# Making one shifted copy of every eighth batch with an adding DMA instead of VectorE

## The chip, the cores and the metric

The kernel runs on one core of a Trainium2 chip. Five engines matter: TensorE (PE in the profile, with its weight loads as PEld), ScalarE (ACT), VectorE (DVE), GpSimd (POOL) and SyncE (SP), which issues most of the DMAs. Each engine works through its own queue in the order in which the program wrote it; an engine whose next instruction waits for a semaphore does nothing else meanwhile. The metric is the device time of one execution in microseconds.

## The reference

Two attention branches read the same input and are mixed by a gate. Only branch A matters for the change: plain softmax attention over 2048 tokens with 32 heads of 16 dimensions.

```python
def _A_ref(x, wqkv, wo):
    B, S, D = x.shape          # 1, 2048, 512
    H = 32; Dh = D // H        # 16
    qkv = (x @ wqkv) ...       # q, k, v: (B, H, S, Dh)
    scores = jnp.einsum("bhqd,bhkd->bhqk", q, k) * (Dh ** -0.5)
    p = _softmax(scores, axis=-1)
    o = jnp.einsum("bhqk,bhkd->bhqd", p, v)
    return o_as_tokens @ wo

g = _sigmoid((x * gate_w).sum(-1, keepdims=True))
a = _A_ref(x, A_wqkv, A_wo)
b = _B_ref(x, B_wqkv, B_w_phi, B_wo)   # linear attention with softmax features
return g * a + (1 - g) * b
```

The work is dominated by the exponentials of branch A: 32 heads x 2048 x 2048 scores.

## The kernel before

**Units, packs and groups.** Branch A is cut into 2048 units: one unit is the score tile of one head for 128 keys and 512 queries (128 x 512 values, one PSUM bank). Four units with the same keys make a pack (four heads on the four strips of the array), 16 packs (2048 keys) make a group, and there are 32 groups of 64 units. For each unit PE makes the scores (`_scores`, L1040), some engine turns them into exponentials, and PE multiplies these with the values and adds the result into the group's accumulator bank (`_values`, L1147). At the end of a group the accumulator is transposed on DVE (L1168) and normalised, and sixteen small DMAs with a transpose behind them (L1191, L1195) put it into `onTA` for the output projection.

**Two ways to an exponential.** Most units (1544 of 2048) go through ACT: scores of two units at a time lie in two of the four ring banks 0 to 3, one ACTIVATE (L1088) makes both exponentials into the ring `ET`, which has `NSLOT` slots of one unit each, and a values matmul (`_pv`) of a whole pack frees its slots. An exponential waits for the values matmul of the unit `NSLOT` places before it.

The other 504 units go through DVE, spread over the groups by the list `NUMS` (6 in the first group, up to 21 in a late one). They are taken in batches of four (`PACK`), 126 in all, by `_vector_batch`. A batch goes like this:

1. Four score matmuls (named `vqk`), each into a free bank of 4 to 7, and per unit one DVE instruction (L946, named `v_bits`) that multiplies by a scale, adds an origin and writes 16-bit integers: read as bf16 these are a first power of two with a straight line between powers. They fill `va[:, 0]`, a tile of 128 x 4 x 512.
2. One DVE instruction (L971 with k = 1, named `v_step`) writes `va[:, 1] = va[:, 0] + 31`, a copy shifted by 31 in the integers, form 128x2048.
3. One DVE instruction (L971 with k = 2) writes `vs[:, :] = va[:, :] + 64`, both halves at once, form 128x4096.
4. Four values groups on PE (named `pvx`), one for each of the four shifted tiles, the first two with `V` and the last two with `V2`, a copy of the values scaled by 0.703125. The sum of the four is the exponential to the precision wanted.

There are two `va` tiles (`NA` = 2, batch number modulo 2) and two `vs` tiles. A batch may write its `va` tile only when the batch two before has been read from it: by its own values groups and by its k = 2 step. A batch is meant to begin seven packs (`LEAD`) before its first unit's turn.

Between these lie the projections of both branches and all of branch B, on PE, DVE, ACT and POOL.

**What sets the order.** A planner (`Plan.order`) simulates the five queues with a cost for each operation (`cost`), a latency until its result is seen elsewhere (`lat`), priorities (`prio`) and times before which it may not run (`rel`). At each step it takes the operation that can start first, and among those about as early the one with the lowest rank. Score matmuls of ACT's units come first on PE. A `pvx` or `pv` becomes urgent some packs after its unit's turn (`URGENT` = 4). PE's gaps are filled with matmuls of a zero tile (L1154). The planner knows that POOL's instructions and certain DVE instructions (`PORT`, among them `v_step`) exclude each other (`o.port`). In `shift`, each operation's priority gets a small random-looking offset that depends on its name, on its running number among operations of that name, and on a list of 34 seeds. The resulting order of every queue is then written out with semaphore waits (`emit`).

All DMAs before the change are issued from SP, except for five from ACT at the start and the end. A large load has a planned cost of 0.5 us on its queue and a latency of its own: 8.0 for `WB`, 4.5 for `WoB`, 4.0 for `WoA`. The sixteen small DMAs of L1191 are one planned operation of 11.0 us on SP.

Of the kernel before, what the change touches and what calls it, by code (L numbers as in the profile page):

```python
# [7 lines left out]
ALU = mybir.AluOpType  # L8
AX = mybir.AxisListType

P = 128
# [4 lines left out]
QCH = 512  # L16
SCALE = float(DH) ** -0.5
F32, BF16 = dt.float32, dt.bfloat16
U16, FP16 = dt.uint16, dt.float16
LOG2E = 1.4426950408889634  # L20
STEPS, RATIO, ORIGIN = (31, 64), 0.703125, 127 * 128 - 279
# [18 lines left out]
class Op:  # L40
    def __init__(self, eng, fn, cost, name, prio, rel, kind, lat):
        self.eng, self.fn, self.cost, self.name = eng, fn, cost, name
        self.prio, self.rel, self.kind, self.lat = prio, rel, kind, lat
        self.deps = []
        self.users = []
        self.left = 0
        self.need = False
        self.acquire = None
        self.release = None
        self.also = None  # L50
        self.twin = None
        self.sem = None
        self.start = self.end = None
        self.on_commit = None
        self.array = 0.0
        self.filler = 0
        self.pad = False
        self.filled = 0
        self.strips = None
        self.urgent = 1 << 30  # L60
        self.held = self.port = False
        self.alone = -99
        self.group = None


class Plan:
# [43 lines left out]
    def op(self, eng, fn, cost, reads=(), writes=(), deps=(), name="", prio=0.0, rel=-99, kind="full",  # L110
           acquire=None, release=None, lat=None, array=None, strips=None, also=None):
        o = Op(eng, fn, cost, name, prio, rel, kind, self.LAT[eng] if lat is None else lat)
        found = {}
        for b in reads:
            for w in b.writers:
                found[id(w)] = w
        for b in writes:
            for w in b.readers or b.writers:
                found[id(w)] = w
            if b.readers:  # L120
                for w in b.writers:
                    found[id(w)] = w
        for d in deps:
            if d is not None:
                found[id(d)] = d
        found.pop(id(o), None)
        o.deps = list(found.values())
        for b in reads:
            b.readers.append(o)
        for b in writes:  # L130
            b.writers, b.readers = [o], []
        o.acquire, o.release, o.also = acquire, release, also
        o.strips = strips
        o.port = eng == "POOL" or eng == "DVE" and name in self.PORT
        o.held = eng == "PE" and acquire is None and name in self.HOLDING
        o.array = cost if array is None else array
        self.ops.append(o)
        return o
# [187 lines left out]
    def emit(self, nc, ctx):  # L326
        sems = {e: ctx.enter_context(nc.semaphore(f"done_{e}")) for e in self.ENGS if e != "SP"}
        for q in self.queues.values():
            for o in q:
                for d in o.deps:  # L330
                    if not (d.eng == o.eng == "PE"):
                        d.need = True
        count = dict.fromkeys(self.ENGS, 0)
        for e, q in self.queues.items():
            for o in q:
                if o.name.startswith("dma"):
                    o.sem = (ctx.enter_context(nc.semaphore(o.name)), 16 * len(o.fn) if isinstance(o.fn, list) else 16)
                elif o.need:
                    count[e] += 1
                    o.sem = (sems[e], count[e])  # L340
# [67 lines left out]
class _Kernel:  # L408
    NRING = 4
    GROUPS = (2, 2)  # L410
    NSLOT = 22
    PACK, PAIRS, PAIR0 = 4, 0, 0
    VCP = 8 * 17
    NQS = 4
# [21 lines left out]
    PADK = 2  # L436
    LAST, FIRST_OUT, NEXT_OUT, DEP_OUT = 0, 3, 0, 2
    ALONE, EARLY = 12, 10
    PVP = 10

    def __init__(self, nc, A_x, A_wqkv, A_wo, B_wqkv, B_w_phi, B_wo, gate_w, out):
# [33 lines left out]
    def _memory(self, ctx):  # L475
        nc, S, NT, NQC = self.nc, self.S, self.NT, self.NQC
# [65 lines left out]
        self.outt = self.WB[:, 0:2, 2 * D:3 * D]  # L542
        tiles = [sb(f"vs{k}", [P, 2, self.PACK, QCH], U16) for k in range(self.NST + self.NA)]
        self.vs, self.va = tiles[:self.NST], tiles[self.NST:]
        self.sbuf_used = at[0]


# [58 lines left out]
    def _consts(self):  # L606
        op = self.plan.op
        B = Buf
        self.b_iden, self.b_mask = B(), B()
        self.b_V = [[B() for _ in range(self.NT // 2)] for _ in range(4)]  # L610
        self.b_V2 = [[B() for _ in range(self.NT // 2)] for _ in range(4)]
        self.early = {}
        self.b_VB = [B() for _ in range(4)]
        op("POOL", lambda e: e.memset(self.iden[:], 0.0), 0.25, writes=[self.b_iden], prio=-90)
        op("POOL", lambda e: e.affine_select(
# [9 lines left out]
        n = 4 * self.NT * self.VCP  # L625
# [294 lines left out]
    def _vector_batch(self, number, units, due):  # L920
# [45 lines left out]
        vs, b_vs, b_vb = self.vs[slot], self.b_vs[slot], self.b_vb[number % self.NA]  # L966
        for k in range(4):
            tile, buf = (vs if k > 1 else va)[:, k % 2], b_vs if k > 1 else b_vb if k else b_va
            if k in (1, 2):
                src, dst = (va[:, 0, 0:n], va[:, 1, 0:n]) if k == 1 else (va[:, :, 0:n], vs[:, :, 0:n])  # L970
                o = op("DVE", lambda e, k=k, src=src, dst=dst: e.tensor_scalar(dst, src, float(STEPS[k - 1]), None,  # L971
                                                                               op0=ALU.add),
                       0.16 + k * n * QCH * 0.00026, reads=[b_va] + [b_vb] * (k - 1), writes=[buf], name="v_step",
                       prio=units[0] / 4 - 4)
                o.urgent = units[0] // 4 - self.AHEAD + 2
            v, bufs = (self.V, self.b_V) if k < 2 else (self.V2, self.b_V2)
            for g in sorted({u // (4 * NT) for u in units}):
# [11 lines left out]
                self.late.setdefault(g, []).append(x)  # L989
                if g in self.opened:  # L990
                    x.deps.append(self.opened[g])

    def _attention(self):
        plan, NT, NQC = self.plan, self.NT, self.NQC
# [704 lines left out]
```

## Time and profile before

| | |
|---|---|
| times of the runs | 757.13 and 758.5 us, median 757.82 |
| span of the profiled execution | 755.8 us, about 2 us less than the median of the runs, since a run's time also has what lies around the span |
| ACT busy | 741.1 us (98%) |
| PE busy | 744.3 us (98%) |
| DVE busy | 719.9 us (95%) |
| POOL busy | 228.6 us (30%) |
| granted clock of TensorE | 1.00 throughout |
| chain that ended last | ACT 69%, PE 18%, DVE 11%, DMA 1% |

A line of the profile names the line of the kernel (L971), the engine, the operation, the tiles written and read (`vs<-vs`; the tiles `va` go by the name `vs` there, since they are allocated from one list), the form (partitions x elements) and a count. Idle time of an engine that isn't the bottleneck costs nothing. Since matmuls overlap, a busy PE is not a PE at its limit. Neighbouring instructions of ACT and DVE overlap a little, so the distance between two starts tells more than a duration.

### The profile page before, as it was taken

Reading aid. Unit: us, or ns where it says so; the run is one execution under the profiler, and the core shown is the slowest. Engines: PE = TensorE matmul, PEld = TensorE weight load, DVE = VectorE, ACT = ScalarE, POOL = GpSimd, SP = SyncE. Lnnn points to the kernel's source line nnn. Section 1 sums busy time; section 2 is a strip of 40 time slices with the busy share of each in tenths; the row PEclk is TensorE's granted clock in tenths of the full one; section 3 lists DMA queues with packets and bytes.
Section 4 is the critical chain, followed back from the end, with each engine's and each line's share of the span. In section 5 each row is a group of like instructions: output and inputs, shape, how many; then the busy total and the mean of one; then the engine's idle time right before and its main releaser. Section 6 shows DMA issues by size and latency. Waiting matters only on the chain.

```text
span 755.8 us, 17204 instructions
## 1 busy us (share of the span) xinstructions
PE 744.3 (98%) x7246; PEld 219.7 (29%) x7246; DVE 719.9 (95%) x1128; ACT 741.1 (98%) x796; POOL 228.6 (30%) x317
## 2 busy tenths in 40 slices
PE   8999999999999999999999999999999999999998
PEld 3323222323332222222232323222232222223222
DVE  4788999999999999999999999999999999999997
ACT  6999999999999999999999999999999999999996
POOL 2213206241534334234407051431615051260010
PEclk9999999999999999999999999999999999999999
DMA  9610000001001000000200312112022103111010
GB/s 220 144 24 6 9 8 6 12 2 15 2 2 15 1 8 10 6 11 3 42 15 19 40 24 48 30 34 39 8 47 33 29 23 44 22 30 28 2 15 29
DMA packets 89181, 20.79 MB, mean 28 GB/s; under 512 B 83472, under 2 KB 88592, under 8 KB 89104
## 3 DMA queue, kind: packets, MB, share of 16 engines
q1 hardware_dynamic: 87232, 18.92, 13.8%
q8 instruction: 56, 0.92, 0.5%
q10 hardware_dynamic: 1872, 0.79, 0.4%
q14 instruction: 21, 0.17, 0.1%
HBM read 4.21 MB, written 2.10 MB: 8 GB/s over the span
## 4 chain that ended last, share of the span: by engine, by line
ACT 69%; PE 18%; DVE 11%; DMA 1%; issue 0%
ACT ET L1088 67%; PE ps L1147 6%; PE ps L1040 6%; DVE vs L946 4%; PE ps L711 4%; DVE vs L971 3%; ACT bq L1335 3%; PE ps L1154 1%; DMA xT<-in_A_x_dram 1%; DVE bq L1332 1%; DVE onB L1500 1%; DVE T L1168 0%; DVE rinvB L1483 0%; DVE btree L1329 0%; DVE btree L1327 0%
## 5 line engine op out<-in xcount | busy, mean ns | idle before, releaser
L1088 ACT ACTIVATE ET<-ps 128x1024 bf16<-128x1024 f32 (+1 forms) x774 | 713.4, 1158 | 1.9 <-PE ps L1040 1.5
L946 DVE TENSOR_SCALAR vs<-ps 128x512 uint16<-128x512 f32 x504 | 323.5, 678 | 12.0 <-PE ps L1040 10.1
L1040 PE MATMUL ps<-qT,kT 32*128 32x512 bf16 (+1 forms) x2052 | 307.3, 384 | 4.1 <-ACT ET L1088 2.0
L971 DVE TENSOR_SCALAR vs<-vs 128x2048 uint16<-128x2048 uint16 (+1 forms) x252 | 241.8, 973 | 1.3 <-PE ps L1147 0.5
L1147 PE MATMUL ps<-vs,V 128*32 128x512 bf16 x2016 | 216.9, 384 | 1.1 <-DVE vs L971 0.7
L1147 PE MATMUL ps<-ET,V 128*32 128x512 bf16 x1544 | 193.8, 387 | 0.4 <-DVE vs L946 0.2
L1040 PEld LDWEIGHTS ps<-qT,kT 32*128 32x128 bf16 x2052 | 76.4, 91 | 300.4 <-ACT ET L1088 287.5
L1339 POOL TENSOR_TENSOR btree<-btree 128x512 f16<-128x512 f16 (+1 forms) x32 | 35.7, 1117 | 208.0 <-DVE btree L1337 207.0
L1147 PEld LDWEIGHTS ps<-ET,V 128*32 128x32 bf16 x1544 | 48.6, 94 | 81.3 <-issue 72.2
L1147 PEld LDWEIGHTS ps<-vs,V 128*32 128x32 bf16 x2016 | 50.1, 95 | 49.9 <-issue 28.0
L711 PE MATMUL ps<-WB,xT 128*128 128x512 bf16 x192 | 58.6, 384 | 0.0
L1154 PE MATMUL ps<-kT,zero 128*32 128x512 bf16 x604 | 58.4, 385 | 0.0
L1324 POOL TENSOR_SCALAR bq<-bq 128x1024 bf16<-128x1024 bf16 x16 | 20.2, 1262 | 105.8 <-DVE bq L1306 64.9
L803 POOL TENSOR_SCALAR qT<-qtmp,mask 128x512 bf16<-128x512 bf16 x30 | 26.7, 897 | 55.6 <-DVE qtmp L798 51.0
L711 PE MATMUL ps<-xT,WA 128*128 128x512 bf16 x120 | 37.1, 384 | 0.3 <-DVE onB L1500 0.3
L1185 POOL TENSOR_TENSOR T<-T,rinv 128x512 bf16<-128x512 f32 x15 | 19.6, 1305 | 55.1 <-DVE rinv L1183 54.9
L1335 ACT ACTIVATE bq<-bq 128x2048 bf16<-128x2048 bf16 x16 | 32.8, 2047 | 0.0
L1168 DVE STREAM_TRANSPOSE T<-ps 128x512 f32<-128x512 f32 x32 | 22.6, 706 | 4.5 <-PE ps L1147 4.4
L1306 DVE CAST bq<-ps 128x512 bf16<-128x512 f32 x32 | 21.6, 679 | 0.7 <-PE ps L711 0.6
L844 POOL TENSOR_SCALAR V<-V 128x544 bf16<-128x544 bf16 x16 | 10.7, 670 | 36.0 <-DVE V L837 35.7
L711 PEld LDWEIGHTS ps<-WB,xT 128*128 128x128 bf16 x192 | 13.1, 97 | 24.8 <-issue 20.5
L1332 DVE TENSOR_TENSOR bq<-bq,btree 128x2048 bf16<-128x2048 bf16 x16 | 19.8, 1240 | 0.0
(91 smaller groups left out, 420.9 us busy)
## 6 DMA issues: line engine op xcount, KB each, us to landing
T<-T SPq DMA_DIRECT2D x240, 8.0 KB, 1.8
WB<-in_B_wqkv_dram SPq DMA_DIRECT2D x1, 1536.0 KB, 8.6
out_dram<-WB SPq DMA_DIRECT2D x12, 128.0 KB, 1.7
WA<-in_A_wqkv_dram SPq DMA_DIRECT2D x2, 384.0 KB, 5.3
WoB<-in_B_wo_dram SPq DMA_DIRECT2D x1, 512.0 KB, 3.9
WoA<-in_A_wo_dram SPq DMA_DIRECT2D x1, 512.0 KB, 4.8
WA<-in_A_wqkv_dram ACTq DMA_DIRECT2D x2, 128.0 KB, 3.3
WA<-in_A_wqkv_dram ACTq DMA_DIRECT2D x1, 256.0 KB, 4.9
```

Of the source, the lines that this page charges most:

```text
L711: return e.matmul(out, lhs, rhs, start=start, stop=stop)
L803: x = self.plan.op("POOL", lambda e, side=side: e.tensor_scalar(self.qT[:, s0 + side, :], tmp, self.mask[:, side:side + 1], 0.0, op0=ALU.m ...
L946: bits = lambda e, to, src: e.tensor_scalar(to, src, SCALE * LOG2E * 128.0, float(ORIGIN), op0=ALU.mult, op1=ALU.add)
L971: o = op("DVE", lambda e, k=k, src=src, dst=dst: e.tensor_scalar(dst, src, float(STEPS[k - 1]), None, op0=ALU.add), 0.16 + k * n * QCH * 0 ...
L1040: return e.matmul(out[:, cols], self.kT[32 * i:32 * i + 32, cp, kt * TOK:(kt + 1) * TOK], self.qT[32 * i:32 * i + 32, s, cols], start=True ...
L1088: o = plan.op("ACT", lambda e: e.activation(self.ET[:, a % NS:a % NS + n, cols], self.ps[:, a % NR:a % NR + n, cols], ACT.Exp, scale=SCALE ...
L1147: ins = e.matmul(self._bank(ot)[32 * i:32 * i + 32, :], v[:, v0:v0 + 32], tile, start=(kt == 0), stop=(kt == self.NT - 1), tile_position=( ...
L1154: ins = e.matmul(self._bank(ot)[32 * i:32 * i + 32, :], self.zero[:], self.kT[:, 0, 0:QCH], start=False, stop=False, tile_position=(0, 32 ...
L1168: t1 = op("DVE", lambda e: e.transpose(T1[:, side].rearrange("p b s -> p (b s)"), src()), 0.735, deps=last, writes=[b_T1[side]], name="n_t ...
L1332: + [("b_sub", two(2048), lambda e: e.tensor_tensor(x, x, spread(tree[:, :, 0]), ALU.subtract))],
L1335: op("ACT", lambda e: e.activation(flat, flat, ACT.Exp), 1.789, reads=[b], writes=[b], name="b_exp", prio=due + 1)
L1339: + [("b_sum", two(128 * n), lambda e, n=n: e.tensor_tensor(half[:, :, 0:n], half[:, :, 0:n], half[:, :, n:2 * n], ALU.add), (n <= self.P_ ...
```

## The change

In batches 8, 16, 24, ... 120 (15 of 126) step 2 above is no longer done by DVE. Instead, a DMA from SP (`fill`) writes the constant 31 into the whole of `va[:, 1]`, from a small tile `steps` of 128 x 512 integers that is read four times, and a DMA from POOL's queue (`add`) adds `va[:, 0]` to it in place, as 16-bit integers. The fill waits for the readers of the batch two before; the add waits for the fill and for the four `v_bits`. Step 3 and the second values group wait for the add. The planner counts 0.6 us on SP and 3.2 us of latency for a fill, 1.1 us on POOL and 5.0 us of latency for an add. The adds share one semaphore that counts on, as do the fills.

The tile `steps` takes 1 KB of each partition, a slot of `ET` also takes 1 KB, and the ring goes from 22 slots to 20. POOL's DMA issues don't count as `port` operations for the planner. `NUMS`, the seeds and all other constants stay.

```diff
-        o.port = eng == "POOL" or eng == "DVE" and name in self.PORT
+        o.port = eng == "POOL" and not name.startswith("dma") or eng == "DVE" and name in self.PORT
...
-                    o.sem = (ctx.enter_context(nc.semaphore(o.name)), 16 * len(o.fn) if isinstance(o.fn, list) else 16)
+                    key = o.stream or o.name
+                    if key not in streams:
+                        streams[key] = [ctx.enter_context(nc.semaphore(key)), 0]
+                    streams[key][1] += 16 * len(o.fn) if isinstance(o.fn, list) else 16
+                    o.sem = tuple(streams[key])
...
-    NSLOT = 22
+    NSLOT = 20
...
+    MOVE0, MOVE = 8, 8
...
+        self.steps = sb("steps", [P, QCH], U16)
...
+        self.b_steps = B()
+        op("POOL", lambda e: e.memset(self.steps[:], STEPS[0]), 0.3, writes=[self.b_steps], prio=-10)
...
         for k in range(4):
             tile, buf = (vs if k > 1 else va)[:, k % 2], b_vs if k > 1 else b_vb if k else b_va
-            if k in (1, 2):
+            if k == 1 and self._moved(number):
+                r = self.dma("SP", f"fill{number}", lambda e, n=n: e.dma_start(
+                    va[:, 1, 0:n], self.steps[:, None, :].to_broadcast([P, n, QCH])), cost=0.6, reads=[self.b_steps],
+                    writes=[b_vb], prio=units[0] / 4 - self.LEAD - 8, lat=3.2)
+                r.stream = f"dma_fill{number % self.NA}"
+                a = self.dma("POOL", f"add{number}", lambda e, n=n: e.dma_start(va[:, 1, 0:n], va[:, 0, 0:n],
+                             accum_op=ALU.add), cost=1.1, reads=[b_va], writes=[b_vb], prio=units[0] / 4 - 4, lat=5.0)
+                a.stream = f"dma_add{number % self.NA}"
+            elif k in (1, 2):
                 src, dst = (va[:, 0, 0:n], va[:, 1, 0:n]) if k == 1 else (va[:, :, 0:n], vs[:, :, 0:n])
                 o = op("DVE", lambda e, k=k, src=src, dst=dst: e.tensor_scalar(dst, src, float(STEPS[k - 1]), None,
                                                                                op0=ALU.add),
...
+    def _moved(self, number):
+        return number >= self.MOVE0 and number % self.MOVE == 0
```

More of the change, by code (lines that the diff above doesn't have):

```diff
@@ L63, in __init__ @@
         self.group = None
+        self.stream = None
 class Plan:
@@ L333, in emit @@
         count = dict.fromkeys(self.ENGS, 0)
+        streams = {}
         for e, q in self.queues.items():
```

## The prediction

> **What bounds the kernel now.** I first looked at each engine's busy time by stage, because shares over the whole span mix the start and the end with the long middle. These are four stretches of the span, each with PE, PEld, DVE, ACT and POOL busy, the granted clock, the DMA share and GB/s:
>
> ```profile
> core 0: us, PE busy (x) PEld busy (x) DVE busy (x) ACT busy (x) POOL busy (x), PEclk, DMA share, GB/s
> 20.00:100.00 80.00, 79.99 (x708) 25.09 (x706) 68.86 (x110) 80.00 (x88) 17.63 (x26) 1.00 0.19 39
> 100.00:400.00 300.00, 298.23 (x2876) 87.54 (x2877) 295.91 (x468) 299.83 (x319) 102.49 (x143) 1.00 0.06 10
> 400.00:660.00 260.00, 256.84 (x2616) 74.08 (x2613) 255.66 (x398) 259.93 (x279) 87.35 (x114) 1.00 0.19 31
> 660.00:747.00 87.00, 85.89 (x919) 23.96 (x916) 85.27 (x129) 86.88 (x95) 15.48 (x19) 1.00 0.10 17
> ```
>
> ACT has work in 80.00 + 299.83 + 259.93 + 86.88 = 726.64 of 727 us. DVE is nearly as full: from 100 on it is idle for 647 - 636.84 = 10.2 us. POOL has room (a third busy), and so have the DMA engines.
>
> Second, the waits of ACT over the whole span (who waited for whom, us in total, times, longest), and third, two pieces of the chain that ended last (start, length, what):
>
> ```profile
> ACT xT L1643 <- PE ps L711: 4.3, 1, 4.3
> ACT qT L770 <- DVE kT L748: 3.2, 1, 3.2
> ACT L668 <- issue: 2.3, 1, 2.3
> ACT ET L1088 <- PE ps L1040: 1.5, 3, 0.7
> ```
>
> ```profile
> 560.88 49.50 ACT ET L1088 x54
> 689.29 55.18 ACT ET L1088 x60
> ```
>
> Three of the four waits lie at the start and the end; for its 774 exponentials ACT waited 1.5 us in all, and never for a values matmul (L1147). One exponential over two score tiles passes every 49.50/54 = 0.917 us to 55.18/60 = 0.920 us. If every one of the 770 wide ones took 0.917 there would be 0.003 x 770 = 2.3 us to win, with the 0.36 us of ACT's idle time 2.7 us. The number of exponentials does not change, so **2.7 us is all that any relief of another engine can bring** before the last exponential, and every late microsecond of ACT is lost for good.
>
> **What is removed.** Groups of instructions by line and form (count, busy us, mean ns, idle before) and the copies' line over the span:
>
> ```profile
> L946 DVE TENSOR_SCALAR vs<-ps 128x512 uint16<-128x512 f32 x504 | 323.5, 678 | 12.0 <-PE ps L1040 10.1
> L971 DVE TENSOR_SCALAR vs<-vs 128x4096 uint16<-128x4096 uint16 x126 | 154.9, 1233 | 0.8 <-PE ps L1147 0.5
> L971 DVE TENSOR_SCALAR vs<-vs 128x2048 uint16<-128x2048 uint16 x126 | 89.1, 713 | 0.5
> L1154 PE MATMUL ps<-kT,zero 128*32 128x512 bf16 x604 | 58.4, 385 | 0.0
> ```
>
> 504 score tiles in batches of four make 126 batches; numbers 8, 16, ... 120 are moved, so 15 copies of form 128x2048 go. The DVE timeline around batch 120 (start, length, merged instructions) shows what one occupies and how a batch runs:
>
> ```profile
> 718.07 1.16 DVE L971 TENSOR_SCALAR vs<-vs 128x4096 uint16<-128x4096 uint16 x1
> 719.14 3.89 DVE L946 TENSOR_SCALAR vs<-ps 128x512 uint16<-128x512 f32 x6
> 722.95 0.68 DVE L971 TENSOR_SCALAR vs<-vs 128x2048 uint16<-128x2048 uint16 x1
> 723.55 1.28 DVE L946 TENSOR_SCALAR vs<-ps 128x512 uint16<-128x512 f32 x2
> 724.75 1.22 DVE L971 TENSOR_SCALAR vs<-vs 128x4096 uint16<-128x4096 uint16 x1
> 725.88 0.68 DVE L1618 COPY xT<-ps 128x512 f32<-128x512 f32 x1
> 726.48 0.68 DVE L971 TENSOR_SCALAR vs<-vs 128x2048 uint16<-128x2048 uint16 x1
> 727.08 1.88 DVE L946 TENSOR_SCALAR vs<-ps 128x512 uint16<-128x512 f32 x3
> ```
>
> The copy starts at 722.95 and the next instruction at 723.55: 0.60 us each, **9.0 us of DVE** in all. DVE was not what ACT waited for, so on the path this is worth 0.
>
> **What is added: a fill and an add.** The trace has neither a DMA that adds nor any from POOL's queue. The nearest issues (KB each, median us from issue to landing):
>
> ```profile
> T<-T SPq DMA_DIRECT2D x240, 8.0 KB, 1.8
> WB<-in_B_wqkv_dram SPq DMA_DIRECT2D x1, 1536.0 KB, 8.6
> WoB<-in_B_wo_dram SPq DMA_DIRECT2D x1, 512.0 KB, 3.9
> WoA<-in_A_wo_dram SPq DMA_DIRECT2D x1, 512.0 KB, 4.8
> ```
>
> The fill writes 128 x 2048 x 2 bytes = 512 KB, like WoB: 3.9 us. It can start once the buffer's last readers are done and runs while the four tiles are made (four times 0.6 us with other work between, 719.14 to 723.03 above), so I cost it at nothing. If that cover goes, because SP is in one of its strings of sixteen small DMAs, it is late by up to 11.13 us:
>
> ```profile
> 720.16 11.13 SPq L1191 DMA_DIRECT2D T<-T  x16
> ```
>
> There are 15 such strings, 167 of 756 us, so about 3 of 15 fills meet one; the planner holds SP for 11.0 us there and places the readers after it, so the order pays, not a stall. Each fill also holds SP some 0.7 us (11.13/16), and whatever stands behind it waits with it: transposes and output stores, which ACT does not wait for.
>
> The add reads 512 KB, reads another 512 KB and writes that. Lower end: one transfer like WoB, 3.9 us. Upper end: three times 512 KB like WB, 8.6 us, plus one wait for DVE (below), 9.5. Between them I take a second read at WB's slope, (8.6 - 3.9)/1024 KB x 512 KB = 2.35 us more: 6.25 us. The planner's own constants are 1.1 + 5.0 = 6.1 us from POOL's turn to landing, and they are no wild guesses elsewhere: 8.5 planned for WB against 8.6, 4.5 for WoA against 4.8, 5.0 for WoB against 3.9. So I take 6.1 us with an error of about +-1.5.
>
> **The added waits.** Two engines wait for the add: DVE before the batch's 128x4096 step, PE before the second of its four value groups. Both queues are in written order, so behind DVE's wait stand the next batch's score tiles and behind PE's wait the score matmuls of ACT. If the add lands as planned, nobody stands: the order puts other work there, and PE has gaps that are filled with 604 zero matmuls (58.4 us). If it lands late by d, PE stands for d. A score group takes PE 0.39 us (below) and may be made while the exponential before it runs, 0.92 us; so about 0.5 us of d is hidden and the rest is ACT's, for good. POOL's own wait for the four tiles delays only its chains, which stand idle for long stretches:
>
> ```profile
> POOL btree L1339 <- DVE btree L1337: 207.0, 16, 25.6
> 412.52 0.39 PE L1040 MATMUL ps<-qT,kT 32*128 32x512 bf16 x2
> ```
>
> My value: one add in three is 1.4 us late and shows 0.9: 5 x 0.9 = **4.5 us**. Ends: 0 (all in time) and 15 x (9.5 - 6.1 - 0.5) = 44 us.
>
> **The buffer is held longer.** Batch 120 has its four tiles by 723.0 at the latest, its big step runs at 724.75, and 1.1 us after that step's end (727.08) the buffer takes its next tiles. With the add, the step waits at least 6.1 us from the last tile instead of the 1.7 us or a little more here: up to 4.4 us longer, some 3 us where the step had to wait anyway, on one of two buffers. DVE can do the other batch meanwhile (four tiles and two steps, 4 x 0.6 + 0.6 + 1.2 = 4.2 us). It has 10.2 + 9.0 = 19.2 us of idle and freed time, 1.3 us per moved batch; I expect about 1 us idle at each, so 0 on the path.
>
> **The ring** of 22 slots becomes 20: exponentials may run ten instead of eleven ahead of the values matmuls, 0.92 us less. ACT never waited for L1147; the planner calls a values group urgent four packs (of four units) after its scores, and in the first group, where only 6 of 64 units leave, 20 slots are 5.5 packs. Ends: 0 and about one exponential, 0.92 us; I take 0.3, early in the run.
>
> **The order** is written anew: the planner's small shifts go by the count of operations of one name, and the copies' count changes from batch 8 on. ACT loses 0.36 us in the present order; another may lose a few us. Ends: -0.4 and +4; I take 0.5.
>
> **The sum.** Span 755.8 + 4.5 + 0.3 + 0.5 = 761.1 us. The runs shown are 757.13 and 758.5, median 757.82, so 2.0 us lie outside the span: **763 us**, 0.7% above.
>
> **Rivals.**
> (1) *Every add is late* (slower). The DMA takes as long as WB's three times 512 KB, 8.6 us: late by 2.5, less 0.5, 2.0 x 15 = 30 us: 757.8 + 30 + 0.8 = 789. It decides from 1.0 us shown per add (15.2 us, 2%), an add of 7.6 us. For it: two queues stand in order behind each add, and ACT has no idle time to give. Against: the planner's constants fit its other DMAs within 0.3 us or are too long. 0.18.
> (2) *DVE becomes the bound.* With 2 us idle per moved batch DVE lacks 30 - 19.2 = 11 us, and the backlog of batches reaches the end: 770; with 3 us, 784. For it: in 660 to 747 DVE has only 1.7 us idle, with two moved batches there. Against: 4.2 us of the other batch cover most of the add. 0.12, half of it above 2%.
> (3) *POOL is shut out by DVE's steps.* The only POOL instruction in 700 to 740 ran beside the step at 718.07:
>
> ```profile
> L1185 POOL TENSOR_TENSOR T<-T,rinv x15: 1055/1059/1909, 79.5 to 718.2; 128x512 bf16<-128x512 f32 x15
> ```
>
> It is the last of fifteen and took, I read, the 1909 ns of the maximum, ending about when the step did; the median is 1059. So an issue on POOL can wait 0.85 us for one step, and for a pair of steps in a row about 2.4. With half of the adds 2.4 late: 7.5 x 1.9 = 14 us, 772. [...] 0.10, half above 2%.
> (4) *A small gain*: all adds land in time and DVE's 9 us tidy the end. At most the 2.7 us: 755 to 757. 0.08.
>
> **Range and chances.** The forecast, with 757 to 769, gets 0.52. The range leaves out the long half of (1) and the deep end of (4): **756 to 786**. Slower by over 2% (above 773; 2% is about what a measurement of this kernel can tell from no change): 0.18 + 0.06 + 0.05 = 0.29. Faster by over 2% (below 742.7) would need 15 us, where the middle has 2.7 to give: 0.01. Within: 0.70.
>
> **What the changed profile would show.** 111 copies of form 128x2048 in place of 126, DVE some 9 us less busy; 15 issues on POOL's queue and 15 fills of 512 KB on SP's. Right: the adds land within 7 us, ACT's waits for L1040 sum to 5 to 10 us. Wrong towards (1) or (3): waits of PE or DVE that end with a DMA into vs, 15 times and 1 us or more each, with ACT waiting on L1040 for tens of us. Towards (2): DVE idle 30 us more, without PE waiting for a DMA, and a longer stretch after the last exponential. A wait of ACT for L1147 would be the ring.

## The result: 8.2% slower, and where the time lies in the profile after

The changed kernel takes 819.41 us (817.52 to 821.3) against 757.82: the ratio is **1.0816 with an interval of 1.0751 to 1.088**. The forecast was 763 us with a range to 786. The profiled execution, the run of 821.3 us, has a span of 819.5 us, 63.7 more than before.

The first view is again the busy time by stretches of the span (PE, PEld, DVE, ACT, POOL, granted clock, DMA share, GB/s):

```profile
core 0: us, PE busy (x) PEld busy (x) DVE busy (x) ACT busy (x) POOL busy (x), PEclk, DMA share, GB/s
20.00:100.00 80.00, 77.89 (x683) 25.37 (x690) 66.01 (x108) 79.80 (x88) 18.01 (x28) 1.00 0.26 50
100.00:400.00 300.00, 291.46 (x2786) 87.03 (x2812) 286.40 (x445) 291.36 (x309) 102.88 (x157) 1.00 0.15 30
400.00:660.00 260.00, 248.44 (x2401) 71.98 (x2423) 232.49 (x357) 242.78 (x259) 80.14 (x109) 0.98 0.26 50
660.00:810.00 150.00, 135.13 (x1318) 37.83 (x1320) 122.47 (x180) 117.00 (x125) 18.56 (x23) 0.91 0.17 34
```

ACT is no longer full. It loses 0.2, 8.6, 17.2 and 33.0 us in the four stretches, where it lost 0.36 in all before. DVE, PE and ACT are all idle more in the same stretches, and the clock is below 1.00 in the last two. Nothing got busy in their place. That is the look of a kernel whose queues wait for each other.

The waits of ACT name what ended them (who waited for whom, us in total, times, longest):

```profile
ACT ET L1109 <- PE ps L1168: 40.3, 6, 10.9
ACT ET L1109 <- PE ps L1061: 16.3, 27, 1.9
ACT xT L1664 <- remote: 8.7, 1, 8.7
```

The lines moved with the change: L1168 is the values matmul (L1147 before), L1061 the scores (L1040), L1109 the exponential (L1088), L956 the score tile on DVE (L946), L989 the copy and the step (L971), L980 the fill, L984 the add, L1212 the string of sixteen small DMAs (L1191). Before, ACT waited never for a values matmul, 1.5 us for scores and 4.3 us at the end. The account of the 63.7 us is 40.3 + (16.3 - 1.5) + (8.7 - 4.3) + 4.3 us that ACT is busy longer (745.4 against 741.1) = 63.8.

The suspect named by the change is the DMA. These are the waits that end with one of the new DMAs on PE and DVE, and beside them DVE's wait for score matmuls:

```profile
PE ps L1168 <- DMA vs<-vs: 4.7, 2, 4.5
DVE vs L989 <- DMA vs<-vs: 4.0, 3, 3.1
DVE vs L956 <- PE ps L1061: 50.4, 77, 3.4
```

An add was late for PE twice and for DVE three times, 8.7 us in all; 4.5 of them are one wait of PE, and its price comes below. DVE stood twelve times as long for scores as for adds; before, that wait was 10.1 us. The groups by form and the DMA issues (KB each, median us from issue to landing) show that the change did what it says:

```profile
L956 DVE TENSOR_SCALAR vs<-ps 128x512 uint16<-128x512 f32 x504 | 326.2, 681 | 52.0 <-PE ps L1061 50.4
L989 DVE TENSOR_SCALAR vs<-vs 128x4096 uint16<-128x4096 uint16 x126 | 158.7, 1264 | 4.8 <-DMA vs<-vs 4.0
L989 DVE TENSOR_SCALAR vs<-vs 128x2048 uint16<-128x2048 uint16 x111 | 78.8, 714 | 0.9
```

```profile
vs<-steps SPq DMA_DIRECT2D x15, 512.0 KB, 3.6
vs<-vs POOLq DMA_DIRECT2D x15, 512.0 KB, 4.8
```

111 copies are left and are 10.3 us less busy; the tiles and steps are 2.7 and 3.8 us busier. The fill lands in 3.6 us and the add in 4.8.

**One stall, from end to end.** ACT's largest wait, read in four short views. First SP's queue (start, length, instructions):

```profile
719.92 11.53 SPq L1212 DMA_DIRECT2D T<-T  x16
731.49 0.66 SPq L980 DMA_DIRECT2D vs<-steps  x1
```

Then the chain that ended last, from the add of batch 112 on:

```profile
735.61 5.86 DMA vs<-vs
741.49 1.23 DVE vs L989
...
748.80 1.24 DVE vs L989
750.08 1.05 PE ps L1168 x6
```

Then the values matmuls of ACT's own units on PE (in brackets the idle time ahead and what ended it), and the exponentials:

```profile
733.00 0.40 PE L1168 MATMUL ps<-ET,V 128*32 128x512 bf16 x4
752.52 0.62 PE L1168 MATMUL ps<-ET,V 128*32 128x512 bf16 x4 [0.84 <-DVE vs L956]
```

```profile
739.46 2.85 ACT L1109 ACTIVATE ET<-ps 128x1024 bf16<-128x1024 f32 x3 [0.21 <-PE ps L1061]
753.18 1.94 ACT L1109 ACTIVATE ET<-ps 128x1024 bf16<-128x1024 f32 x2 [10.87 <-PE ps L1168]
```

The fill is issued the moment the string ends, the add follows it, and the step of the batch follows the add. Behind them come the last values groups of an old accumulator, and only then may the values matmuls of the next group of units begin. From 733.00 to 752.52 none of those runs, so no slot of the ring comes free, the 20 slots fill, and ACT stands from 742.3 to 753.2. **The ring is where a late batch shows; the lateness is made earlier, in the batch.** All long stalls lie at the opening of a group, each behind such a pause of the values matmuls of ACT's units: 6.9 us at 279.7, 2.9 at 499.5, 8.1 at 645.3, 10.9 at 742.3, 10.8 at 774.7. The chains ahead of them differ. Over the 20 us and more before the end of each of the first three no fill and no add stands on the chain. Ahead of the last one both do, with no string before the fill, and PE stands 4.5 us for the add:

```profile
771.39 4.42 DMA vs<-steps
...
776.35 4.78 DMA vs<-vs
```

In the stall at 742.3 the fill is late behind a string, and in the one at 774.7 fill and add are on the chain, so the DMA seems guilty after all. Two theories follow. **The order**: the planner, given another list of operations, writes another order of all queues, to which the seeds and `NUMS` are not fitted, and that order lets batches come late with or without a DMA. **The DMA**: the shorter ring, the fill, the add and the longer hold of the buffer make the stalls, and the order only passes them on.

### The profile page after: what moved, and what is told of

It is laid out like the page before. It is cut to its first block, busy times and chain, and to the rows that moved or that the text cites. A ratio compares the mean times of both kernels' runs of the same rounds, so it can differ in the third digit from the quotient of the medians.

```text
span 819.5 us, 17422 instructions
## 1 busy us (share of the span) xinstructions
PE 773.9 (94%) x7312; PEld 230.4 (28%) x7379; DVE 721.7 (88%) x1113; ACT 745.4 (91%) x796; POOL 225.7 (28%) x333
## 4 chain that ended last, share of the span: by engine, by line
ACT 52%; PE 28%; DVE 16%; DMA 3%; issue 1%; DVEq 0%; POOLq 0%
ACT ET L1109 49%; PE ps L1168 10%; PE ps L1061 10%; DVE vs L956 6%; DVE vs L989 5%; PE ps L721 3%; PE ps L1175 3%; ACT bq L1356 3%; DMA vs<-vs 1%; DMA vs<-steps 1%; DVE T L1189 1%; DVE onB L1521 1%; DMA xT<-in_A_x_dram 1%; DMA WT<-onB 0%; PE ps L1081 0%
## 5 line engine op out<-in xcount | busy, mean ns | idle before, releaser
L1109 ACT ACTIVATE ET<-ps 128x1024 bf16<-128x1024 f32 (+1 forms) x774 | 716.5, 1116 | 57.3 <-PE ps L1168 40.3
L956 DVE TENSOR_SCALAR vs<-ps 128x512 uint16<-128x512 f32 x504 | 326.2, 681 | 52.0 <-PE ps L1061 50.4
L1061 PE MATMUL ps<-qT,kT 32*128 32x512 bf16 (+1 forms) x2052 | 326.4, 388 | 14.9 <-ACT ET L1109 9.1
L989 DVE TENSOR_SCALAR vs<-vs 128x2048 uint16<-128x2048 uint16 (+1 forms) x237 | 236.7, 1006 | 5.7 <-DMA vs<-vs 4.0
L1168 PE MATMUL ps<-vs,V 128*32 128x512 bf16 x2016 | 214.1, 391 | 12.4 <-DMA vs<-vs 4.7
L1168 PE MATMUL ps<-ET,V 128*32 128x512 bf16 x1544 | 196.9, 393 | 2.3 <-DVE vs L956 2.0
L1061 PEld LDWEIGHTS ps<-qT,kT 32*128 32x128 bf16 x2052 | 80.1, 91 | 312.9 <-ACT ET L1109 266.7
L1168 PEld LDWEIGHTS ps<-ET,V 128*32 128x32 bf16 x1544 | 49.9, 95 | 81.1 <-issue 68.3
L1175 PE MATMUL ps<-kT,zero 128*32 128x512 bf16 x716 | 71.8, 404 | 0.0
L1168 PEld LDWEIGHTS ps<-vs,V 128*32 128x32 bf16 x2016 | 49.8, 95 | 70.1 <-issue 36.7
L721 PE MATMUL ps<-WB,xT 128*128 128x512 bf16 x164 | 51.3, 384 | 3.1 <-issue 2.4
L984 POOL DMA_DIRECT2D vs<-vs x15 | 14.2, 947 | 89.0 <-DMA vs<-steps 58.4
L721 PE MATMUL ps<-xT,WA 128*128 128x512 bf16 x100 | 31.6, 383 | 1.2 <-issue 1.0
L1189 DVE STREAM_TRANSPOSE T<-ps 128x512 f32<-128x512 f32 x32 | 22.7, 709 | 10.8 <-PE ps L1168 10.7
L1175 PEld LDWEIGHTS ps<-kT,zero 128*32 128x32 bf16 x716 | 17.8, 96 | 26.8 <-issue 24.8
```

The costliest lines, as they stand in the source:

```text
L721: return e.matmul(out, lhs, rhs, start=start, stop=stop)
L956: bits = lambda e, to, src: e.tensor_scalar(to, src, SCALE * LOG2E * 128.0, float(ORIGIN), op0=ALU.mult, op1=ALU.add)
L1061: return e.matmul(out[:, cols], self.kT[32 * i:32 * i + 32, cp, kt * TOK:(kt + 1) * TOK], self.qT[32 * i:32 * i + 32, s, cols], start=True ...
L1109: o = plan.op("ACT", lambda e: e.activation(self.ET[:, a % NS:a % NS + n, cols], self.ps[:, a % NR:a % NR + n, cols], ACT.Exp, scale=SCALE ...
L1168: ins = e.matmul(self._bank(ot)[32 * i:32 * i + 32, :], v[:, v0:v0 + 32], tile, start=(kt == 0), stop=(kt == self.NT - 1), tile_position=( ...
L1175: ins = e.matmul(self._bank(ot)[32 * i:32 * i + 32, :], self.zero[:], self.kT[:, 0, 0:QCH], start=False, stop=False, tile_position=(0, 32 ...
```

## The experiments

Each kernel ran beside the kernel before on the same chip (757.4 to 757.7 us); ratios are to that.

**The ring alone.** The kernel before with 20 slots.

```diff
-    NSLOT = 22
+    NSLOT = 20
```

> The kernel before with 20 ring slots instead of 22 and nothing else. In the changed kernel ACT waits 40.3 us for values matmuls (L1168), which it never did before, and those free the ring's slots. If the shorter ring by itself is the cause: 790 to 800 us, with waits of ACT for a values matmul of 7 to 11 us. If the ring is only where a stall of PE becomes visible: within 2 us of the kernel before, 756 to 760, and no such wait over 1 us.

Measured 757.97 us, ratio 1.0002 (0.9993 to 1.0012), as expected if the ring only shows a delay. ACT still never waits for a values matmul; its only wait before an exponential is:

```profile
ACT ET L1088 <- PE ps L1040: 1.9, 3, 1.1
```

The planner's order with 20 slots is almost that of before, and so is the time: two slots less cost nothing there. A new plan does not have to lose time.

**The order alone.** The kernel before, with DVE still making every copy. Only the name of the copies that the change moves is another. So the running numbers of `v_step`, and with them the planner's small shifts, change as they do in the changed kernel; no DMA is added and the ring keeps 22 slots.

```diff
-    PORT = ("v_step", "b_neg",
+    PORT = ("v_step", "v_c", "b_neg",
...
-                        name="v_step",
+                        name="v_c" if k == 1 and number >= 8 and number % 8 == 0 else "v_step",
```

> The kernel before, 22 slots, no DMA, no fill: VectorE makes every copy, but in batches 8, 16, ... 120 the copy has another name for the planner, so that the running number of all other steps goes on as it does in the changed kernel and their small offsets differ. No instruction is added, removed or changed in size; only the order differs. Theory F (the loss is that of an order fitted by seeds to one count of operations): 790 to 810 us, with ACT waiting tens of us for values matmuls. Rival H (the loss comes from the add, the fill and the buffer held longer): 757 to 760, ACT waiting under 3 us for its exponentials.

Measured **808.61 us, ratio 1.0671 (1.0648 to 1.0693)**, with no operation added or taken away. ACT's waits, DVE's largest group and the last stretch have the changed kernel's look:

```profile
ACT ET L1088 <- PE ps L1147: 35.9, 5, 16.0
ACT xT L1643 <- PE ps L711: 11.5, 1, 11.5
```

```profile
L946 DVE TENSOR_SCALAR vs<-ps 128x512 uint16<-128x512 f32 x504 | 324.2, 679 | 42.2 <-PE ps L1040 39.8
```

```profile
660.00:800.00 140.00, 130.88 (x1220) 36.45 (x1232) 120.00 (x180) 108.25 (x116) 17.99 (x22) 0.91 0.10 15
```

The stalls on the ring, DVE's waits for scores (39.8 us) and even the lower clock need no DMA. A renaming alone makes 51 us, against the changed kernel's 61.6; 11.5 - 4.3 = 7.2 of them are the later end.

**Any other order?** Perhaps the renaming hit on a bad order. Three more orders of the kernel before were tried, each without a change in the work: one of the planner's costs moved by 0.1 ns, other seeds drawn at random, and all seeds zero. In these three, and in all pairs below, the final output projection of the last tile also takes a bank outside the score ring (`RINGOUT = 0`). That edit concerns only the end of the run; on the chip it was not run alone.

```diff
-    RINGOUT = 1
+    RINGOUT = 0
...
-        return 0.0634 + n * 0.000833
+        return 0.0635 + n * 0.000833
```

> The kernel before, with the planner's cost of an ACT instruction raised by a tenth of a nanosecond (0.0634 to 0.0635 us) and the last output tile in a free bank. No instruction changes, no offset changes, no count changes; only the order that the planner finds. Theory F1 (the fitted order falls apart at any change of what the planner sees, however small): 780 to 810 us. Theory F2 (it is the shift of the running numbers of the steps, so of their offsets, that costs): 757 to 760. Rival H: 757 to 760.

```diff
-    SEEDS = (3340, 7601, 0, 849, 2310, 7659,
+    SEEDS = (2202, 9326, 1034, 4180, 1932, 8118,
```

> The kernel before with 34 other seeds, drawn at random (and the last output tile in a bank of the free four instead of the ring's). No DMA for copies. Theory F: the fitted seeds are worth 30 to 45 us, so 785 to 805. Rival H: 757 to 762, since seeds only break ties among operations that are about equally urgent.

```diff
-    SEEDS = (3340, 7601, 0, 849, 2310, 7659,
+    SEEDS = (0,) * 34
```

> The kernel before with all 34 seeds zero, so no offsets at all (and the last output tile in a free bank). Theory F: an order that nobody fitted, 785 to 805 us. Rival H: 757 to 762.

| order of the kernel before | us | ratio (95%) | end that the planner foresees, us |
|---|---|---|---|
| cost of ACT + 0.1 ns | 799.89 | 1.0558 (1.0527 to 1.0588) | 790.4 |
| random seeds | 796.7 | 1.0513 (1.0492 to 1.0534) | 790.0 |
| seeds zero | 803.24 | 1.0602 (1.0564 to 1.064) | 795.6 |
| copies renamed (above) | 808.61 | 1.0671 (1.0648 to 1.0693) | 801.2 |

The last column is no measurement. It is the latest end that `Plan.order` gives an operation, worked out from each kernel's code without the chip. For the kernel before it is 753.2 us, with or without the edit of `RINGOUT`, and for the changed kernel 803.7. So most of the loss stands in the plan already; the measured times lie 7 to 10 us above it in these four orders, 5 in the kernel before and 16 in the changed one.

The waits of ACT in the first of them:

```profile
ACT ET L1088 <- PE ps L1147: 18.0, 4, 6.3
ACT xT L1643 <- PE ps L711: 15.4, 2, 15.1
```

The stalls on the ring are there in each (18.0, 20.8, 28.2 and 35.9 us). The first one's span is 42.3 us longer; of these at most 15.4 - 4.3 = 11.1 may come from the edit at the end, and the other 31 lie before it. Four orders that were not fitted average 802.1 us, some 45 above the fitted one. It is not the renaming's shifts that are bad: each of these four edits gave up 5 to 7%, and none changed the work.

**The change between orders of one kind.** If an unfitted order costs some 45 us, the change's own price has to be read between two unfitted orders. The changed kernel with the same random seeds, and with zero seeds (the seed edits of above, made to the changed kernel):

> The changed kernel with the same 34 random seeds as other_before (and the same bank for the last output tile). The difference to other_before is what fill, add and the shorter ring do to an order that fits neither kernel. Theory F: 5 to 25 us above other_before, so most of the 61 us is not theirs. Rival H: 50 to 65 us above other_before.

> The changed kernel with all 34 seeds zero (and the last output tile in a free bank), the partner of zero_before. The pair of random seeds gave 24 us for fill, add and shorter ring on an unfitted order. If that is the price of the change itself: 15 to 30 us above zero_before. If the 24 us were as much the luck of two orders: anywhere from 5 us below to 30 above.

Measured 820.41 us (1.0826, 1.0798 to 1.0854) and 808.45 us (1.0671, 1.064 to 1.0702). Against their partners that is 820.41 - 796.7 = 23.7 and 808.45 - 803.24 = 5.2 us; the changed kernel itself against the renamed copies is 819.41 - 808.61 = 10.8. Every difference points the same way, but the orders scatter by as much as the differences are large. ACT's waits on the ring were 20.8 us with random seeds and 28.2 with zero seeds; with the change they are 33.8 and 34.5.

**A shorter add.** The changed kernel with every queue's order as it is, but each add moves one of the batch's four tiles. The second copies of the other three tiles are left at 31, so this kernel leaves out a part of the computation.

```diff
-                a = self.dma("POOL", f"add{number}", lambda e, n=n: e.dma_start(va[:, 1, 0:n], va[:, 0, 0:n],
+                a = self.dma("POOL", f"add{number}", lambda e, n=n: e.dma_start(va[:, 1, 0:1], va[:, 0, 0:1],
```

> The changed kernel with every queue in the same order and every wait in place, but each add moves only the first of the four tiles (128 KB in place of 512 KB; the other three second copies are left at 31, so a part of the computation is left out). The add should land some 1 to 2 us sooner. Theory F: the loss is written into the order, 815 to 820 us, within 5 us of the changed kernel. Rival H (the add's duration is what PE and DVE stand for): 15 times 1 to 2 us less, 790 to 805.

Measured 812.82 us (809.88 and 815.76), ratio 1.0728 (1.0635 to 1.0822). That lies between the two expectations (815 to 820 and 790 to 805), nearer to the first. The add, the end of the two last stalls, and a piece of the chain ahead of the first of these two:

```profile
vs<-vs POOLq DMA_DIRECT2D x15, 128.0 KB, 2.8
```

```profile
753.26 1.94 ACT L1109 ACTIVATE ET<-ps 128x1024 bf16<-128x1024 f32 x2 [10.38 <-PE ps L1168]
783.26 1.94 ACT L1109 ACTIVATE ET<-ps 128x1024 bf16<-128x1024 f32 x2 [8.45 <-PE ps L1168]
```

```profile
740.23 0.70 DVE vs L956
740.96 1.83 DVE vs L989 x2
```

Fifteen adds that land 2.0 us sooner are 30 us in all. They brought 6.6, with intervals that overlap, and the waits on the ring fell by 2.0 us, from 40.3 to 38.3. The two stalls that had a DMA on their chain now differ. In the first one the add no longer stands on the chain, which runs through a score tile and the steps of DVE; the stall stays, 10.4 us for 10.9, so it does not hang on the add in this order. The second one falls from 10.8 to 8.5 us, about what the add is shorter: this one hangs on fill and add. The length of the add is not what most of the stalls hang on.

**The DMA without a new order.** The counterpart: the fitted order of before, as planned with 20 slots, is kept, the 15 copies are taken out of DVE's queue, and fill and add are put into the queues of SP and POOL at the places that their times in that plan give. The other edits of the change (tile `steps`, streams, `_moved`) are as in its diff.

```diff
+                if k == 1 and self._moved(number):
+                    self.swaps.append((o, number, va, n, list(parts)))
...
+    def _swap(self):
+        q = self.plan.queues
+        at = {}
+        for o, number, va, n, bits in self.swaps:
+            f = Op("SP", lambda e, va=va, n=n: e.dma_start(
+                va[:, 1, 0:n], self.steps[:, None, :].to_broadcast([P, n, QCH])), 0.6, f"dma_fill{number}", 0, -99, "full", 3.2)
+            a = Op("POOL", lambda e, va=va, n=n: e.dma_start(va[:, 1, 0:n], va[:, 0, 0:n], accum_op=ALU.add),
+                   1.1, f"dma_add{number}", 0, -99, "full", 5.0)
...
+            a.start = a.end = o.start
...
+            q["DVE"].remove(o)
+            for x, e in ((f, "SP"), (a, "POOL")):
+                q[e].insert(next((i for i, y in enumerate(q[e]) if y.start >= x.start), len(q[e])), x)
```

> The order of the kernel before (with 20 slots, which cost nothing) is kept instruction by instruction, and the 15 copies are taken out of VectorE's queue; a fill and an add as in the changed kernel are put into SP's and POOL's queues where the copies' turn was. Whoever needs a copy stands in its queue until the add has landed. Theory F (a fitted order with slack of 0.5 us): the add is there about 5.7 us after its turn instead of 0.7, so 5 us late at each of 15 places, less the 0.5 us that a score group may be late: up to 68 us, 800 to 830; if the ring of score banks and the groups' rest hide more, 765 to 800. Rival H' (only a new order hurts, the DMA as such is hidden): 757 to 765.

Measured **861.74 us, ratio 1.1374 (1.1327 to 1.1421)**, granted clock 0.937 on the mean. Waits of ACT, PE and DVE:

```profile
ACT ET L1127 <- PE ps L1079: 100.7, 50, 11.2
PE ps L1186 <- DMA vs<-vs: 66.2, 13, 11.0
DVE vs L982 <- DMA vs<-vs: 69.9, 14, 8.1
```

Here the signs named for a late add are all there: waits that end with the DMA 13 and 14 times, 66.2/13 = 5.1 and 69.9/14 = 5.0 us each, and ACT waiting for scores (L1079 here), not for the ring. By the prediction's rule, that all of a wait but 0.5 us is ACT's, the 13 waits of PE are 13 x 4.6 = 60 us; the kernel lost 104, more than any expectation. ACT's wait for scores is 100.7 of it. How much of the rest is the lower clock, and how much the waits of DVE, was not tried. The adds are late here partly because their fills are: POOL stood 103.6 us for fills, at 9 of the 15 adds. So late copies are dear where the order makes no room for them, and the planner's new order in the changed kernel did make room: 8.7 us of waiting are left of 15 adds.

**Away from the edge.** If the order costs so much because DVE is full, both prices should go when DVE has room. The two kernels with zero seeds, and each entry of `NUMS` two smaller: 440 instead of 504 units on DVE, 64 more on ACT, which is 32 exponentials or 32 x 0.92 = 29 us more for ACT. 13 batches are moved.

```diff
-    NUMS = (6, 10, 16, 14, 14, 16, 16, 19, 13, 19, 17, 12, 17, 11, 19, 19, 14, 20, 12, 16, 19, 13, 17, 16, 15, 20, 12, 20, 17, 21, 21, 13)
+    NUMS = (4, 8, 14, 12, 12, 14, 14, 17, 11, 17, 15, 10, 15, 9, 17, 17, 12, 18, 10, 14, 17, 11, 15, 14, 13, 18, 10, 18, 15, 19, 19, 11)
```

> The kernel before with no offsets (seeds zero) and two units fewer per group on VectorE, 440 in place of 504; the last output tile in a free bank. ACT gets 64 units more, 32 exponentials of 0.917 us: 29 us more of ACT. Theory F with VectorE's edge as its reason (504 units are so many that only a fitted order keeps VectorE's batches from being late): the stalls mostly go and it runs at ACT's pace, 785 to 793 us, faster than zero_before (803) although ACT has more to do. If the unfitted order costs its 40 us whatever VectorE has to do: 825 to 835.

> The changed kernel with no offsets and 440 units, partner of light_before. If fill and add cost time only through VectorE's late batches: within 5 us of light_before, 785 to 797, and 20 us faster than the changed kernel. If each add stalls PE or ACT by itself: 15 to 30 us above light_before.

Measured 790.31 us (1.0431, 1.0401 to 1.0462) and 791.82 us (1.0451, 1.0376 to 1.0527). ACT alone would need 757.8 + 29 = 787. The changed one's waits and a middle stretch of it:

```profile
ACT ET L1109 <- PE ps L1168: 1.2, 1, 1.2
DVE vs L989 <- DMA vs<-vs: 1.1, 2, 0.9
```

```profile
100.00:400.00 300.00, 292.24 (x2737) 86.26 (x2738) 261.94 (x407) 299.08 (x318) 99.37 (x146) 1.00 0.14 28
```

With DVE busy 262 of 300 us instead of 296, the unfitted order costs little and the DMA nothing that shows: 32 us above 757.8 where ACT's extra work alone is 29, 1.5 us between the two (two runs of the changed one lie 4.8 us apart), ACT full. And both are faster than the same seeds with *more* work taken off ACT (803.24 and 808.45): in an order that nobody fitted, giving DVE the last 64 units loses time.

**Equal fitting.** Last, both kernels with seeds fitted anew, in the same manner (stage by stage, by the end that the planner itself foresees) and with the same number of trial orders, some 10,700 each.

```diff
-    SEEDS = (3340, 7601, 0, 849, 2310, 7659,
+    SEEDS = (3340, 7841, 1128, 2695, 9066, 3442,
...
-    RINGOUT = 1
+    RINGOUT = 0
```

> The kernel before with seeds fitted anew, stage by stage, by some 10,700 trial orders of the planner on its own terms (time of ACT and number of VectorE's tiles done at the end of each stage); the last output tile in a free bank. It shows how far so short a fitting comes: 763 to 772 us, against 797 to 803 for orders that nobody fitted.

```diff
-    SEEDS = (3340, 7601, 0, 849, 2310, 7659,
+    SEEDS = (6560, 6457, 6044, 5860, 1785, 1108,
...
-    RINGOUT = 1
+    RINGOUT = 0
```

> The changed kernel (fill, add, 20 slots, 504 units) with seeds fitted in the same way and with as many trials as fit_before. If all of the loss is the lost fit: within 5 us of fit_before. If fill and add also cost VectorE's batches time while VectorE is at its edge: 10 to 22 us above fit_before, 777 to 790, and still some 30 us faster than the changed kernel with its old seeds.

Measured 766.86 us (1.0123, 1.0093 to 1.0152) and 782.02 us (1.0323, 1.0293 to 1.0353). ACT's main waits of the kernel before, refitted, and of the changed one, refitted:

```profile
ACT ET L1088 <- PE ps L1147: 2.4, 1, 2.4
ACT xT L1643 <- PE ps L711: 10.5, 1, 10.5
```

```profile
ACT ET L1109 <- PE ps L1168: 15.4, 2, 10.1
ACT xT L1664 <- PE ps L721: 9.2, 1, 9.2
```

Refitting alone takes the changed kernel from 819.4 to 782.0: 37 of its 61.6 us were a lost fit that a search can find again. The old kernel, refitted, is within 9.1 us of its best, 6.2 of them the later end (10.5 against 4.3). What stays between the two is **15.2 us**, the price of the change with 504 units on DVE, of which 15.4 - 2.4 = 13.0 us are stalls on the ring. The planner foresees this too: its own ends are 762.2 and 778.1 us.

How the 15.2 us divide between the ring's two slots, the fills, the add and the longer hold of the buffer was not tried. Late fills are hardly in it. POOL's wait for fills ahead of its adds, in the changed kernel and in the refitted one:

```profile
POOL vs L984 <- DMA vs<-steps: 58.4, 7, 17.7
```

```profile
POOL vs L984 <- DMA vs<-steps: 1.5, 2, 0.9
```

In the refitted one the waits of PE and DVE that end with an add are 0.5 and 0.9 us, and no fill or add stands on the chain ahead of its two stalls (5.3 us at 716.4, 10.1 at 741.5). The DMAs are in time; the batches are late all the same. One pair of searches is also one draw: it gives a size, not a second figure. No version here beats the kernel before.

## Why the prediction was wrong, point by point

**What bounds the kernel: right, and read too narrowly.** ACT was the bound, 2.7 us the most to win, and every us that it stands is lost. But the same table showed DVE idle for only 10.2 us of 647 and PE as full. The prediction read from this that relief of another engine wins little. That DVE and PE had nothing to give either stood in the same rows.

**The step that failed: "The order ... Ends: -0.4 and +4; I take 0.5."** This is the term that was put far too low. Measured without any part of the change but the shifts, it is +51 us, and four orders lie 39 to 51 above the fitted one. The prediction saw that the shifts are numbered anew and took the present order's quality, 0.36 us lost, for what the planner delivers. It is what a choice among very many orders delivered. The rows hinted at it: a DVE with 1.7 us idle in the last 87 has little room for a batch that comes a few us later. The plan said it outright: its own end, which needs no chip, goes from 753.2 to 803.7 us with the change, 50.5 of the 61.6 us.

**The second step: "the order pays, not a stall", "so 0 on the path".** For the fill, for the longer hold of the buffer and for the order's reaction the prediction booked nothing, since the planner would place the readers later. It does, and where DVE is full that is not free: the change's own price is 15 us with equal fitting, 5 to 24 in the other pairs with 504 units, and none that shows with 440. Which of these terms, or the ring's two slots, makes the 15 us stays open. The estimate that 3 of 15 fills meet an SP string took the two as independent (and 15 x 11.13 = 167 us is a little high; the fifteen strings before sum to 163). In the changed kernel 7 of the 15 adds stood for their fill. Strings come every two groups, about 49 us, and moved batches about every 49 us too, so a meeting can repeat.

**The add: right within its error.** From the start of POOL's issue to landing it took 4.8 us (4.5 to 5.9), 0.88 of them on POOL; forecast 6.1 +- 1.5. The waits that end with an add, 8.7 us in all, are nearer to "one in three 1.4 us late" (7 us of standing) than to every add late, while in the run with the old order kept the rule for d came out too low, 60 us for 104.

**The removed copies: right in size.** 9.0 us forecast, 10.3 us less of that form. That they are worth nothing on the path was not measured by itself.

**The ring: right as a term in the order of before, wrong as a sign.** The ratio of 1.0002 is 0.15 us, not clear of nothing; forecast 0.3. What two slots cost in an order that is not fitted was not tried. And "a wait of ACT for L1147 would be the ring" misleads: 40.3 us of such waits came, and also in kernels with 22 slots. A wait at a buffer names where a delay arrives, not where it is made.

**The rivals.** (1) Every add late: no, 2 + 3 waits instead of 15, though its price is real when the order is held (104 us). (2) DVE as the bound: its sign came, DVE idle 97.8 us against 36 while PE waits little for a DMA. But 50.4 us of the idle time are waiting for scores, and the renamed copies, without any DMA, have 39.8 us of the same wait. (3) POOL shut out by DVE's steps: no. The issues of the adds, with minimum, median and maximum in ns:

```profile
L984 POOL DMA_DIRECT2D vs<-vs x15: 872/883/1547, 95.2 to 776.4; - x15
```

The median is within 11 ns of the fastest. The worst costs 0.7 us; it met two steps of DVE and ended 0.12 us after them:

```profile
735.61 1.55 POOL L984 DMA_DIRECT2D vs<-vs  x1 [15.72 <-DMA vs<-steps]
```

```profile
735.08 1.96 DVE L989 TENSOR_SCALAR vs<-vs 128x2048 uint16<-128x2048 uint16 x2
```

Five other issues ran beside a step and took 0.88 to 0.98 us. L1185 in the profile before shows what a step can cost POOL: ten of its fifteen instructions, which met none or only the first 0.02 us of one, took 1.06 us each; the five beside a step took 1.37 to 1.91 and ended 0.90 to 0.92 us after it. So the exclusion that the planner counts with shows in this line. Of the issues of the adds one in fifteen was held up, and the longest landing was 5.9 us against a median of 4.8. (4) A small gain: no.

No rival said that the order itself could be lost, and so nothing in the range, which ended at 786, stood for it.

## What to carry to other kernels

Where the order of the queues was found by a search and an engine runs without idle time, the old time is the best of many draws. Before a forecast, let the planner work out its own end for both kernels. Then re-plan the *old* kernel with a change that means nothing (a renaming, other seeds, a cost off by 0.1 ns), and compare the new kernel with that too, not only with the best old time. Judge a change of the work with equal fitting on both sides, or at a load at which no second engine is full. And follow a wait at a ring back to what keeps its slots, before sizing the ring.

## What the runs showed of the hardware

**The clock fell twice without a long gap.** The granted clock was 1.00 throughout before. In the changed kernel it went to 0.50 in three stretches before the end, from 592.0 for 10.2 us, from 749.0 for 6.8 and from 779.7 for 20.5: three, two and six times 3.4 us. The stretch of 3.4 us ahead of the first, and then a window in the first, across the end of the second and inside the third (columns as in the first table):

```profile
588.60:592.00 3.40, 2.14 (x15) 0.57 (x11) 3.40 (x7) 3.40 (x4) 0.68 (x1) 1.00 0.06 11
592.00:603.00 11.00, 10.91 (x59) 2.02 (x61) 6.22 (x10) 7.30 (x9) 5.31 (x8) 0.53 0.01 1
754.00:760.00 6.00, 6.00 (x61) 1.89 (x53) 2.90 (x5) 4.06 (x6) 0.00 (x0) 0.85 0.01 3
786.00:800.00 14.00, 14.00 (x87) 2.34 (x80) 5.47 (x7) 8.57 (x9) 0.00 (x0) 0.50 0.05 11
```

In the first PE is busy 2.14 of 3.40 us (63%), with no single gap over 1.07 us. The second fall came behind a gap of 1.41 us at most; the third came 3.1 us into a wait of PE for an add, 4.52 us long, that ended at 781.17. In the other three windows PE is full and ACT stands: 11 - 7.30 = 3.7, 6 - 4.06 = 1.9 and 14 - 8.57 = 5.4 us, 11 us, of the size of the 14.8 us that its waits for scores grew by. If the idle time ahead is what lowers the clock, which no run shows, it was paid twice here, once while PE stood and once at the lower clock after it; no run separates the two.

**The adding DMA.** 512 KB added in place in SBUF landed in 4.8 us (4.5 to 5.9), 128 KB in 2.8 (2.6 to 3.6): 384 KB more take 2.0 us, and by the line through the two points, an estimate, some 2.1 us of both do not depend on the size. A fill of 512 KB from a tile read four times took 3.6 us (3.3 to 5.4). The add was dearer than the fill by 1.2 us, less than the 2.35 that the prediction took from `WB`.
